# Strassen's seven products for the first product of a mixture-of-experts layer

## The chip, the cores and the metric

The kernel runs on one core of a Trainium2 chip. The metric is the device time of one execution, in microseconds (us). A core has a matrix engine (TensorE, PE in the profile, with its weight loads as PEld), a vector engine (VectorE, DVE), an activation engine (ScalarE, ACT), GpSimd (POOL), and SyncE (SP), whose queue issues most of the DMA transfers. Matmuls write to PSUM, which has eight banks; VectorE and ScalarE take the results from there to SBUF.

## The reference

Attention over pooled keys gives 2304 tokens of 512 features; a first gated layer follows, and then the second layer, which the change is about:

```python
def _moe2_ref(x, w_gate, w1, w2) -> np.ndarray:
    N, D = x.shape
    E = w_gate.shape[1]
    logits = x @ w_gate
...
    for _ in range(8):
        P /= P.sum(1, keepdims=True) + 1e-09
        P /= P.sum(0, keepdims=True) + 1e-09
        P *= N / E
    out = np.zeros((N, D), dtype=np.float32)
    for e in range(E):
        h = np.maximum(x @ w1[e], 0.0)
        ye = h @ w2[e]
        out += P[:, e:e + 1] * ye
    return out.astype(np.float32)
```

N is 2304, D is 512, there are E = 8 experts, and the hidden width F is 1024. All experts see all tokens. The first product is `x @ w1[e]`, the second `h @ w2[e]`.

## The kernel before, in words

Every float32 product is made of three passes. An operand is held as `hi + lo`, and `PASSES` names hi·hi, hi·lo and lo·hi. Making such a pair takes one ScalarE copy (hi) and one subtraction on VectorE or GpSimd (lo).

Tokens are cut into `NBLK` = 6 blocks of `TB` = 384, each of `TPB` = 3 tiles of 128. The program's order is written out by hand: each engine works through its own queue in the order of the code, and waits at an instruction hold up all that is behind it on that engine.

**First layer** (line 665 on, 72 steps): while it runs, attention goes on in stages, and the first two blocks also round the weights from float64. After each block, `x2_step` (lines 548 to 578) leaves the layer's result in `x2[j]`, and `gate_logits` (lines 583 to 603) makes the second layer's gate logits from it, in stages: one ScalarE copy and one GpSimd subtraction over 1536 columns, twelve small matmuls, three transposes.

**Second layer** (lines 794 to 828): 48 units, (expert e, block j) with the expert outside, and in each eight steps f, one for 128 hidden features; 384 steps. A step makes the first product for 384 tokens in one `gv` bank (12 matmuls of 384 columns: four slices of D, three passes, line 270), then ScalarE's Relu (line 806) and VectorE's rest (line 807), and the second product of the step before, in three `big` banks (9 matmuls of 512 columns, line 764), which is summed in PSUM over all eight f. At a unit's end three VectorE instructions (line 779) add the result, times the token's weight, to `acc`. `stream` loads weight chunks on SP's queue and splits them (lines 240 and 245); each is loaded once. `split_x` (lines 615 and 616) splits the next unit's block of `x2` anew.

The gate's softmax and its eight rounds of normalisation (`sinkhorn`, lines 714 to 748) are one stage per step of the first two units. A round has two halves: a product with `ones` on TensorE (line 739) sums over the partitions, and nine VectorE instructions stand between one such product and the next.

Of the kernel before, what the change touches and what calls it, by code (L numbers as in the profile page):

```python
# [8 lines left out]
F32 = mybir.dt.float32  # L9
# [10 lines left out]
def attention_moe_moe_kernel(  # L20
# [27 lines left out]
    E, _, FF2 = moe2_w1.shape  # L48
# [9 lines left out]
    TB = 384  # L58
# [4 lines left out]
    NF2 = FF2 // 128  # L63
    ROUNDS = 8
# [4 lines left out]
    base = ctx.enter_context(tc.tile_pool(name="base", bufs=1))  # L69
# [13 lines left out]
    x2 = {j: const.tile([128, KT, TB], F32, name=f"x2_{j}") for j in range(2)}  # L83
# [5 lines left out]
    def cols_of(w, f):  # L89
        return w[:, f * 128 : (f + 1) * 128].rearrange("(k p) f -> p k f", p=128)  # L90

    def rows_of(w, f):
        return w[f * 128 : (f + 1) * 128, :]
# [25 lines left out]
    NWA = 8  # L119
    wsplit = {}  # L120
# [9 lines left out]
    def load_wide():  # L130
# [5 lines left out]
        t = base.tile([128, KT * TB], U32, tag="x2", name="wide", bufs=NWIDE)  # L136
# [53 lines left out]
    def source(i):  # L190
        """Of a chunk of the first layer: its number among the rounded, and whether it
        is that one's first use."""
        kind, j, f = chunks[i][0]
        return 3 * f + "gvo".find(kind), j == 0

    def load_chunk():
        """Loads the next chunk that is not rounded on the way."""
# [11 lines left out]
        if i < n_moe1:
            nc.sync.dma_start(out=t, in_=narrow[source(i)[0]])  # L210
        elif kind == "1":
            nc.sync.dma_start(out=t.rearrange("p (k f) -> p k f", f=128), in_=cols_of(w, f))
        else:
            nc.sync.dma_start(out=t, in_=rows_of(w, f))
# [3 lines left out]
    def split_chunk():  # L218
        """Splits the next chunk; False where there is none, or no room for it."""
# [3 lines left out]
        m, first = source(i) if i < n_moe1 else (None, False)  # L223
# [5 lines left out]
        if i >= n_moe1 and (i - n_moe1) % (2 * NF2) < 2 * NF2 - NWA:  # L229
# [3 lines left out]
        if pool is None or in_use[tag] >= bufs:  # L233
            return False
# [633 lines left out]
```

## Time and profile before

| | |
|---|---|
| runs | 2297.35 us median of three, 2296.33 to 2297.91 |
| profiled execution | span 2291.2 us; its own time is not listed apart from the span. The median of the runs is 6.2 us above the span |
| TensorE busy | 96 % of the span, 11453 matmuls |
| VectorE, ScalarE, GpSimd busy | 40 %, 29 %, 15 % |
| granted TensorE clock, mean | 0.979 of 2.4 GHz |
| start of the second layer | its first product starts at about 670 us |

The page gives each engine's busy time, and then the span in 40 slices with a digit for the busy share in tenths. A stage table gives the same for stretches that one chooses. In the timeline a line is an instruction or a merged run of equal ones: start, duration, engine, source line, operation, output and inputs, and in brackets how long the engine had been idle and what ended that. Matmuls are pipelined, so that the distance between starts, and not the duration shown for one, is what a matmul costs.

### The profile page before, as it was taken

Reading aid. Unit: us, or ns where it says so; the run is one execution under the profiler, and the core shown is the slowest. Engines: PE = TensorE matmul, PEld = TensorE weight load, DVE = VectorE, ACT = ScalarE, POOL = GpSimd, SP = SyncE. Lnnn points to the kernel's source line nnn. Section 1 sums busy time; section 2 is a strip of 40 time slices with the busy share of each in tenths; the row PEclk is TensorE's granted clock in tenths of the full one; section 3 lists DMA queues with packets and bytes.
Section 4 is the critical chain, followed back from the end, with each engine's and each line's share of the span. In section 5 each row is a group of like instructions: output and inputs, shape, how many; then the busy total and the mean of one; then the engine's idle time right before and its main releaser. Section 6 shows DMA issues by size and latency. Waiting matters only on the chain.

```text
span 2291.2 us, 28161 instructions
## 1 busy us (share of the span) xinstructions
PE 2189.2 (96%) x11453; PEld 2002.6 (87%) x11453; DVE 919.0 (40%) x1510; ACT 663.8 (29%) x1342; POOL 351.3 (15%) x258
## 2 busy tenths in 40 slices
PE   4668899999999999999999999999999999999999
PEld 3657789999998999999999999999999999999998
DVE  7877965543345223224222322422332242223222
ACT  5345455544442122113111211311221131112111
POOL 5645635544530000000000000000000000000000
PEclk7779899999999999999999999999999999999999
DMA  8554444333340001002000100200020020001111
GB/s 220 152 164 151 138 118 124 116 119 106 121 134 14 1 22 52 1 1 74 1 1 19 56 1 1 74 1 1 15 59 1 1 74 1 1 15 33 28 28 28
DMA packets 115858, 129.77 MB, mean 57 GB/s; under 512 B 26384, under 2 KB 71440, under 8 KB 115728
## 3 DMA queue, kind: packets, MB, share of 16 engines
q1 hardware_dynamic: 110544, 118.53, 17.7%
q10 hardware_dynamic: 5184, 9.44, 1.1%
q8 instruction: 89, 1.46, 0.3%
q14 instruction: 41, 0.34, 0.0%
HBM read 113.79 MB, written 14.16 MB: 56 GB/s over the span
## 4 chain that ended last, share of the span: by engine, by line
PE 88%; DVE 6%; issue 2%; ACT 2%; POOL 1%; DMA 1%; SPq 0%; ACTq 0%; POOLq 0%; DVEq 0%
PE gv L270 46%; PE big L764 35%; PE big L558 5%; DVE made L174 1%; DVE sum L324 1%; PE at L398 1%; DVE wa_lo L245 1%; POOL wa_lo L245 1%; PE at L270 1%; DVE made L173 1%; PE at L469 1%; DVE wide L177 0%; PE at L455 0%; DMA kv<-in_k_dram 0%; DVE g L693 0%
## 5 line engine op out<-in xcount | busy, mean ns | idle before, releaser
L270 PE MATMUL gv<-xs,wa_hi 128*128 128x384 f32 x2688 | 701.6, 342 | 18.8 <-DVE g L693 9.6
L807 DVE SCALAR_TENSOR_TENSOR h<-gv,h 128x384 fp32r<-128x384 f32 x384 | 214.0, 557 | 1041.5 <-ACT h L806 1041.0
L806 ACT ACTIVATE h<-gv 128x384 fp32r<-128x384 f32 x384 | 188.9, 492 | 1202.3 <-PE gv L270 1202.3
L270 PEld LDWEIGHTS gv<-xs,wa_hi 128*128 128x128 f32 x2688 | 493.5, 191 | 41.3 <-issue 11.1
L270 PE MATMUL gv<-xs,wa_lo 128*128 128x384 f32 x1344 | 457.2, 340 | 11.4 <-POOL wa_lo L245 8.9
L270 PE MATMUL gv<-xs,wb_hi 128*128 128x384 f32 x1536 | 393.1, 336 | 0.0
L764 PE MATMUL big<-wb_hi,h 128*128 128x512 f32 x1152 | 389.9, 392 | 0.0
L764 PE MATMUL big<-wa_hi,h 128*128 128x512 f32 x1152 | 389.7, 392 | 0.0
L270 PEld LDWEIGHTS gv<-xs,wb_hi 128*128 128x128 f32 x1536 | 282.0, 188 | 16.4
L270 PEld LDWEIGHTS gv<-xs,wa_lo 128*128 128x128 f32 x1344 | 255.9, 190 | 13.1 <-POOL wa_lo L245 9.9
L270 PE MATMUL gv<-xs,wb_lo 128*128 128x384 f32 x768 | 259.1, 337 | 0.0
L764 PEld LDWEIGHTS big<-wa_hi,h 128*128 128x128 f32 x1152 | 216.1, 188 | 40.4
L764 PEld LDWEIGHTS big<-wb_hi,h 128*128 128x128 f32 x1152 | 216.3, 188 | 40.2
L764 PE MATMUL big<-wb_lo,h 128*128 128x512 f32 x576 | 227.5, 395 | 0.0
L764 PE MATMUL big<-wa_lo,h 128*128 128x512 f32 x576 | 227.5, 395 | 0.0
L245 DVE TENSOR_TENSOR wa_lo<-stage,wa_hi 128x512 fp32r<-128x512 f32 x148 | 134.4, 920 | 77.1 <-ACT wa_hi L240 65.4
L245 POOL TENSOR_TENSOR wa_lo<-stage,wa_hi 128x512 fp32r<-128x512 f32 x96 | 142.3, 1506 | 115.8 <-ACT wa_hi L240 102.3
L558 PE MATMUL big<-h,wa_hi 128*128 128x384 f32 x576 | 150.8, 342 | 0.3 <-DVE h L697 0.3
L240 ACT ACTIVATE wa_hi<-stage 128x512 fp32r<-128x512 f32 x244 | 140.8, 622 | 34.6 <-PE big L764 33.6
L270 PEld LDWEIGHTS gv<-xs,wb_lo 128*128 128x128 f32 x768 | 144.0, 188 | 0.0
L764 PEld LDWEIGHTS big<-wb_lo,h 128*128 128x128 f32 x576 | 108.0, 187 | 18.2
L764 PEld LDWEIGHTS big<-wa_lo,h 128*128 128x128 f32 x576 | 108.0, 187 | 18.2
(136 smaller groups left out, 1696.0 us busy)
## 6 DMA issues: line engine op xcount, KB each, us to landing
stage<-narrow SPq DMA_DIRECT2D x180, 256.0 KB
stage<-in_moe_w_dram SPq DMA_DIRECT2D x128, 256.0 KB
narrow<-made ACTq DMA_DIRECT2D x36, 256.0 KB
wide<-in_moe_w_gate_dram SPq DMA_DIRECT2D x12, 512.0 KB
wide<-in_moe_w_val_dram SPq DMA_DIRECT2D x12, 512.0 KB
wide<-in_moe_w_out_dram SPq DMA_DIRECT2D x12, 512.0 KB
kv<-in_k_dram SPq DMA_DIRECT2D x16, 288.0 KB
qraw<-in_q_dram SPq DMA_DIRECT2D x24, 192.0 KB
```

What stands on the lines that cost most here:

```text
L173: nc.vector.tensor_scalar(out=x, in0=high, scalar1=0x80000000, scalar2=None, op0=ALU.bitwise_and)
L174: nc.vector.scalar_tensor_tensor(out=x, in0=high, scalar=3, in1=x, op0=ALU.logical_shift_left, op1=ALU.bitwise_or)
L240: nc.scalar.activation(out=hi, in_=raw, func=AF.Copy)
L245: eng.tensor_tensor(out=lo, in0=raw, in1=f32(hi), op=ALU.subtract)
L270: nc.tensor.matmul(out=out_, lhsT=a[s], rhs=b[m], start=(i == 0), stop=(i == n - 1))
L324: nc.vector.tensor_reduce(out=s, in_=t.rearrange("p h j d -> p h d j"), axis=AX.X, op=ALU.add)
L398: nc.tensor.matmul(out=pt[:RP, 2 * i * SP : 2 * (i + 1) * SP], lhsT=qt[r][:, hp], rhs=kb[:, hp].rearrange("p i s -> p (i s)"), start=True, ...
L469: nc.tensor.matmul(out=po[64 * i : 64 * i + 64, h // 2 - 2 * g], lhsT=vs[:, h], rhs=a_ts[u][:, h].rearrange("p r s -> p (r s)"), start=Tru ...
L558: nc.tensor.matmul(out=x2p[d][:, :TB], lhsT=w[s][:, d * 128 : (d + 1) * 128], rhs=gs[j, f][m], start=(first and i == 0), stop=(last and i ...
L764: nc.tensor.matmul(out=yp[n][t], lhsT=a[s][:, cs], rhs=w[m], start=(f == 0 and i == 0), stop=(f == NF2 - 1 and i == 2),)
L806: nc.scalar.activation(out=hi, in_=pt[:, :TB], func=AF.Relu)
L807: nc.vector.scalar_tensor_tensor(out=lo, in0=pt[:, :TB], scalar=0.0, in1=f32(hi), op0=ALU.max, op1=ALU.subtract)
```

## The change

The second layer's loops are turned around: three pairs of token blocks outside, then the experts, then q = 0 to 3, which names a pair of hidden slices (q and q + 4): 96 steps instead of 384. In a step the first product is a 2 by 2 block product: hidden slice (`fh`) by half of D on the weights' side, half of D by block of tokens on the other. It is computed with one level of Strassen's algorithm (in Winograd's form): seven products of 6 matmuls of 384 columns, P1 to P7, instead of eight.

- **Tokens' side:** `after_block` takes the place of `gate_logits`. After an odd block it also makes three sums of blocks and splits them; seven split operands per pair of blocks go to DRAM (`fx_store`), and come back when the pair is worked on (`load_xf`, 768 KB each): for the next pair, each right after its operand's last product in the pair before.
- **Weights' side:** `prep_w1` makes, in every step, four sums on GpSimd (256 columns each), splits three blocks and four sums on ScalarE and GpSimd; `prep_w2` splits two slices of w2 on ScalarE and VectorE. All weights are loaded and split again for each pair: 1 MB per step. On the host, w1 is laid out so that a step's four blocks are contiguous.
- **Results:** P1, then P1+P6, P1+P6+P7 and P1+P6+P7+P4 are summed in one `at` bank, read in between by ScalarE copies (`c1`, `c2`) and a VectorE sum; three VectorE additions combine the others. A step makes four hidden tiles.
- **Second product:** six `y_chunk`s of 6 matmuls of 512 columns, of the step before, stand between the products. Each ends in a VectorE instruction that adds to `acc`, in every step and no longer once per expert.
- **Order:** `slot2` stands seven times in a step, and emits a stage of the gate or of `sinkhorn`, one of `prep_w1` and one of `prep_w2`. In step 0 there is no second product yet. `more` is a pool on the memory of `base`, which ends there.

```diff
+    NPAIR = NBLK // 2
+    CPP = 2 * TPB
+    QF = NF2 // 2
+    FX = 4 * TB
...
+    def fx_tile(dtype, name):
+        return xring.tile([128, 2, 2, TB], dtype, tag="fx", name=name, bufs=NWIDE)
+    def fx_split(src, eng):
+        t = fx_tile(F32R, "fx")
+        nc.scalar.activation(out=t[:, 0], in_=src, func=AF.Copy)
+        eng.tensor_tensor(out=t[:, 1], in0=src, in1=f32(t[:, 0]), op=ALU.subtract)
+        return t
+    def fx_store(t, p, i):
+        nc.sync.dma_start(out=xd[p][i], in_=f32(t).rearrange("p s k c -> p (s k c)"))
...
+    def after_block(j):
+        p, odd = divmod(j, 2)
+        fx = [fx_split(x2[j][:, 0:2], nc.gpsimd)]
+        yield
+        fx.append(fx_split(x2[j][:, 2:4], nc.gpsimd))
+        yield
+        pt = side_bank()
+        mm(
+            pt[:E, :TB],
+            [
+                ((wg_hi[:, kk], wg_lo[:, kk]), tuple(fx[kk // 2][:, s, kk % 2] for s in range(2)))
...
+        )
         nc.vector.tensor_copy(out=lt, in_=pt[:E, :TB])
...
+        if odd:
+            fx_store(fx[1], p, 2)
+        else:
+            fx_store(fx[0], p, 0)
+            fx_store(fx[1], p, 1)
...
+        if not odd:
             return
...
+        yield "logits"
+        a, b = x2[j - 1], x2[j]
+        tt = fx_tile(F32, "tt")
+        sub = nc.vector.tensor_sub
+        sub(out=tt[:, 0], in0=b[:, 0:2], in1=a[:, 0:2])
+        sub(out=tt[:, 1], in0=b[:, 2:4], in1=tt[:, 0])
+        yield
+        t1 = fx_split(tt[:, 0], nc.gpsimd)
+        yield
+        t2 = fx_split(tt[:, 1], nc.gpsimd)
+        fx_store(t1, p, 3)
+        yield
...
+        t4 = fx_split(tt[:, 1], nc.gpsimd)
...
+        t3 = fx_split(tt[:, 0], nc.gpsimd)
+        fx_store(t4, p, 5)
...
+        fx_store(t3, p, 6)
...
+    steps2 = [(p, e, q) for p in range(NPAIR) for e in range(E) for q in range(QF)]
...
+    def load_w1(n):
...
+            raw1[n] = pools["late"].tile([128, 4, 2, 128], F32, tag="raw1", name="raw1", bufs=2)
+            nc.sync.dma_start(out=raw1[n].rearrange("p a k f -> p (a k f)"), in_=moe2_w1[e, q])
+    def load_w2(n):
...
+            raw2[n] = pools["more"].tile([128, 2, DM], F32, tag="raw2", name="raw2", bufs=2)
+            nc.sync.dma_start(
+                out=raw2[n], in_=moe2_w2[e].rearrange("(h g p) d -> g p h d", h=2, p=128)[q]
+            )
+    def prep_w1(n):
...
+        raw = raw1.pop(n)
+        pool = pools["more" if n % 2 else "late"]
+        a11, a12, a22, a21 = (raw[:, i] for i in range(4))
+        ss = pools["late"].tile([128, 4, 2, 128], F32, tag="ss", name="ss", bufs=1)
+        s1, s2, s4, s3 = (ss[:, i] for i in range(4))
+        pl = nc.gpsimd.tensor_tensor
+        fa = pool.tile([128, 2, 3, 2, 128], F32R, tag="fa", name="fa", bufs=1)
+        fs = pool.tile([128, 2, 4, 2, 128], F32R, tag="fs", name="fs", bufs=1)
+        wsum[n] = fa, fs
+        nc.scalar.activation(out=fa[:, 0], in_=raw[:, 0:3], func=AF.Copy)
+        pl(out=s1, in0=a21, in1=a22, op=ALU.add)
+        pl(out=s3, in0=a11, in1=a21, op=ALU.subtract)
+        yield
+        pl(out=s2, in0=s1, in1=a11, op=ALU.subtract)
+        pl(out=s4, in0=a12, in1=s2, op=ALU.subtract)
+        yield
+        nc.scalar.activation(out=fs[:, 0], in_=ss, func=AF.Copy)
+        pl(out=fa[:, 1], in0=raw[:, 0:3], in1=f32(fa[:, 0]), op=ALU.subtract)
+        yield
+        pl(out=fs[:, 1, 0:2], in0=ss[:, 0:2], in1=f32(fs[:, 0, 0:2]), op=ALU.subtract)
+        pl(out=fs[:, 1, 2:4], in0=ss[:, 2:4], in1=f32(fs[:, 0, 2:4]), op=ALU.subtract)
+        yield
+    def prep_w2(n):
...
+        t = pools["more"].tile([128, 2, 2, DM], F32R, tag="w2hl", name="w2hl", bufs=2)
+        w2hl[n] = t
+        for i in range(2):
+            nc.scalar.activation(out=t[:, 0, i], in_=raw[:, i], func=AF.Copy)
+            nc.vector.tensor_sub(out=t[:, 1, i], in0=raw[:, i], in1=f32(t[:, 0, i]))
+            yield
...
+    def load_xf(p, i):
+        if p < NPAIR:
+            xf[p, i] = pools["late"].tile([128, 2, 2, TB], F32R, tag=f"xf{i}", name=f"xf{i}", bufs=1)
+            nc.sync.dma_start(out=f32(xf[p, i]).rearrange("p s k c -> p (s k c)"), in_=xd[p][i])
...
                 pools["late"] = ctx.enter_context(tc.tile_pool(name="late", bufs=1, reuse_waits="tile"))
+                load_w1(0)
+                load_w1(1)
+                first_w = prep_w1(0)
+            if j == NBLK - 1 and 2 <= f < 9:
+                load_xf(0, (0, 3, 4, 2, 6, 1, 5)[f - 2])
+            if j == NBLK - 1 and f >= NF1 - 4:
+                next(first_w, None)
...
-                    gate = gate_logits(prev[0])
+                    gate = after_block(prev[0])
...
-            if j == NBLK - 1 and f >= NF1 - KT:
-                split_x(0, f - NF1 + KT)
...
+        PRODUCTS = {
+            "P1": ((0, 0), 0),
+            "P2": ((0, 1), 1),
+            "P3": ((1, 2), 2),
+            "P4": ((0, 2), 5),
+            "P5": ((1, 0), 3),
+            "P6": ((1, 1), 4),
+            "P7": ((1, 3), 6),
+        }
+        def product(n, name, pt, start):
+            (which, i), x = PRODUCTS[name]
+            w = wsum[n][which]
+            t = xf[steps2[n][0], x]
+            m = 0
+            for k in range(2):
+                for s, o in PASSES:
                     nc.tensor.matmul(
-                        out=yp[n][t],
-                        lhsT=a[s][:, cs],
-                        rhs=w[m],
-                        start=(f == 0 and i == 0),
-                        stop=(f == NF2 - 1 and i == 2),
+                        out=pt[:, :TB],
+                        lhsT=w[:, s, i, k],
+                        rhs=t[:, o, k],
+                        start=(start and m == 0),
+                        stop=(m == 5),
+                        skip_group_check=True,
                     )
...
+        def hidden(n, fh, half, src):
+            t = pools["more"].tile([128, 2, TB], F32R, tag=f"h{fh}{half}", name=f"h{fh}{half}", bufs=2)
+            hs[n, fh, half] = t
+            nc.scalar.activation(out=t[:, 0], in_=src, func=AF.Relu)
+            nc.vector.scalar_tensor_tensor(
+                out=t[:, 1], in0=src, scalar=0.0, in1=f32(t[:, 0]), op0=ALU.max, op1=ALU.subtract
             )
...
+        def y_chunk(n, t):
...
+            p, e, q = steps2[n]
+            half, i = divmod(t, TPB)
+            cs = slice(i * 128, (i + 1) * 128)
+            py = bank("big", 4)
+            m = 0
+            for fh in range(2):
+                h = hs[n, fh, half]
+                for s, o in PASSES:
+                    nc.tensor.matmul(
+                        out=py, lhsT=h[:, s, cs], rhs=w2hl[n][:, o, fh], start=(m == 0), stop=(m == 5)
+                    )
+                    m += 1
...
+            if e == 0 and q == 0:
+                acc[t] = pools["more"].tile([128, DM], F32, tag="acc", name="acc", bufs=CPP + 2)
+                if p == 0:
+                    nc.vector.tensor_copy(out=acc[t], in_=py)
+                else:
+                    nc.vector.tensor_scalar_mul(out=acc[t], in0=py, scalar1=pr)
+            elif e == 0 and p == 0:
+                nc.vector.tensor_tensor(out=acc[t], in0=py, in1=acc[t], op=ALU.add)
+                if q == QF - 1:
+                    unscaled.append((t, pr))
...
+                while unscaled:
+                    u, pu = unscaled.pop(0)
+                    nc.vector.tensor_scalar_mul(out=acc[u], in0=acc[u], scalar1=pu)
+                nc.vector.scalar_tensor_tensor(
+                    out=acc[t], in0=py, scalar=pr, in1=acc[t], op0=ALU.mult, op1=ALU.add
+                )
+            if (e, q) == (E - 1, QF - 1):
+                for p0, np_, rows in out_rows(tt * 128):
+                    nc.sync.dma_start(out=rows, in_=acc[t][p0 : p0 + np_])
...
+        for n, (p, e, q) in enumerate(steps2):
+            last_of_pair = (e, q) == (E - 1, QF - 1)
+            pa = bank("at", 2)
+            pc = bank("gv", 2)
+            pb = bank("gv", 2)
+            product(n, "P1", pa, True)
+            if n == 0:
+                product(n, "P5", pc, True)
+                x2_step(*prev)
+                base_pool.__exit__(None, None, None)
+                pools["more"] = ctx.enter_context(
...
+                )
+                load_w2(0)
+                gate = after_block(NBLK - 1)
+                sk = sinkhorn()
+            load_w2(n + 1)
+            load_w1(n + 2)
+            prep = prep_w1(n + 1)
+            prep2 = prep_w2(n)
+            def slot2():
+                global_stage()
+                next(prep, None)
+                next(prep2, None)
+            def global_stage():
+                if n < QF + 2:
+                    if not sk_on:
+                        if next(gate, None) == "logits":
+                            sk_on.append(True)
+                    elif next(sk, "end") == "end":
+                        next(gate, None)
+            c1 = c_tile()
+            nc.scalar.copy(out=c1, in_=pa[:, :TB])
...
+            y_chunk(n - 1, 3)
+            slot2()
+            if n > 0:
+                product(n, "P5", pc, True)
+            c5 = c_tile()
+            nc.scalar.copy(out=c5, in_=pc[:, :TB])
...
+            y_chunk(n - 1, 4)
+            slot2()
+            product(n, "P6", pa, False)
+            c2 = c_tile()
...
+            y_chunk(n - 1, 5)
+            slot2()
+            product(n, "P3", pc, False)
+            nc.vector.tensor_tensor(out=pc[:, :TB], in0=pc[:, :TB], in1=c2, op=ALU.add)
+            hidden(n, 0, 1, pc[:, :TB])
...
+            slot2()
+            product(n, "P7", pa, False)
+            nc.vector.tensor_tensor(out=c5, in0=pa[:, :TB], in1=c5, op=ALU.add)
+            hidden(n, 1, 1, c5)
...
+            y_chunk(n - 1, 0)
+            slot2()
+            product(n, "P2", pb, True)
+            nc.vector.tensor_tensor(out=pb[:, :TB], in0=pb[:, :TB], in1=c1, op=ALU.add)
+            hidden(n, 0, 0, pb[:, :TB])
...
+            y_chunk(n - 1, 1)
+            slot2()
+            product(n, "P4", pa, False)
+            hidden(n, 1, 0, pa[:, :TB])
...
+            y_chunk(n - 1, 2)
+            slot2()
+        for t in (3, 4, 5, 0, 1, 2):
+            y_chunk(len(steps2) - 1, t)
...
+        if name == "moe2_w1":
+            a = a.reshape(8, 2, 2, 128, 2, 4, 128).transpose(0, 5, 3, 4, 1, 2, 6)
+            a = np.stack([a[:, :, :, f, k] for f, k in ((0, 0), (0, 1), (1, 1), (1, 0))], axis=3)
+            a = np.ascontiguousarray(a.reshape(8, 4, 128, 1024))
```

## Rows read from the trace of the kernel before

**Rows 1.** The page: span, busy times, and the slices of two rows

```profile
span 2291.2 us, 28161 instructions
PE 2189.2 (96%) x11453; PEld 2002.6 (87%) x11453; DVE 919.0 (40%) x1510; ACT 663.8 (29%) x1342; POOL 351.3 (15%) x258
...
POOL 5645635544530000000000000000000000000000
PEclk7779899999999999999999999999999999999999
```

**Rows 2.** Stage table: start, end and length, each engine's busy time (count), clock, DMA

```profile
200.00:300.00 100.00, 80.81 (x467) 76.27 (x466) 87.05 (x115) 50.78 (x93) 60.11 (x40) 0.88 0.47 145
...
1200.00:1600.00 400.00, 400.00 (x2008) 362.50 (x2007) 120.06 (x211) 85.47 (x176) 0.00 (x0) 1.00 0.07 22
```

**Rows 3.** Timeline of TensorE in the second layer: where each group of matmuls begins

```profile
1301.66 0.39 PE L764 MATMUL big<-wa_hi,h 128*128 128x512 f32 x1
...
1303.75 0.51 PE L270 MATMUL gv<-xs,wa_hi 128*128 128x384 f32 x2
...
1305.85 0.39 PE L764 MATMUL big<-wa_hi,h 128*128 128x512 f32 x1
...
1307.93 0.51 PE L270 MATMUL gv<-xs,wa_hi 128*128 128x384 f32 x2
```

**Rows 4.** Waits from 720 us on: us in total, times, longest

```profile
ACT h L806 <- PE gv L270: 1171.2, 373, 3.7
DVE h L807 <- ACT h L806: 1031.8, 369, 3.6
```

**Rows 5.** Groups by line: busy us, mean ns of one, idle before

```profile
L807 DVE SCALAR_TENSOR_TENSOR h<-gv,h 128x384 fp32r<-128x384 f32 x384 | 214.0, 557 | 1041.5 <-ACT h L806 1041.0
L806 ACT ACTIVATE h<-gv 128x384 fp32r<-128x384 f32 x384 | 188.9, 492 | 1202.3 <-PE gv L270 1202.3
...
L615 ACT ACTIVATE xs<-x 128x384 fp32r<-128x384 f32 x192 | 99.0, 516 | 0.0
...
L779 DVE SCALAR_TENSOR_TENSOR acc<-big,prob,acc 128x512 f32<-128x512 f32 x126 | 86.5, 742 | 1.7 <-PE big L764 1.7
...
L245 DVE TENSOR_TENSOR wb_lo<-stage,wb_hi 128x512 fp32r<-128x512 f32 x64 | 44.0, 692 | 33.8 <-ACT wb_hi L240 33.8
...
L240 ACT ACTIVATE wb_hi<-stage 128x512 fp32r<-128x512 f32 x64 | 39.7, 627 | 33.6 <-PE big L764 33.6
...
L587 POOL TENSOR_TENSOR xs<-x,xs 128x1536 fp32r<-128x1536 f32 x6 | 21.0, 3498 | 50.0 <-ACT xs L586 50.0
...
L577 ACT COPY x<-big 128x384 f32<-128x384 f32 x16 | 7.3, 480 | 2.8 <-PE big L558 2.6
...
L573 DVE TENSOR_TENSOR x<-x,big 128x384 f32<-128x384 f32 x8 | 3.9, 545 | 0.0
```

**Rows 6.** Timeline of POOL and of DVE in the first layer, around 400 us

```profile
400.80 0.46 POOL L327 TENSOR_TENSOR sum<-kv 72x128 f32<-72x128 f32 x1
401.22 5.01 POOL L245 TENSOR_TENSOR wa_lo<-stage,wa_hi 128x512 fp32r<-128x512 f32 x4
...
400.81 5.97 DVE L245 TENSOR_TENSOR wa_lo<-stage,wa_hi 128x512 fp32r<-128x512 f32 x1 [0.68 <-POOL kv L327]
```

**Rows 7.** Timeline of one half round of the normalisation, on PE and DVE

```profile
703.46 0.28 PE L739 MATMUL at<-cs,ones 128*128 128x8 f32 x2
...
707.84 0.28 PE L739 MATMUL at<-cs,ones 128*128 128x8 f32 x2
...
703.77 0.17 DVE L740 TENSOR_SCALAR cs<-at 128x8 f32<-128x8 f32 x1 [1.06 <-PE at L739]
...
705.95 0.44 DVE L736 TENSOR_REDUCE cs<-prob 128x8 f32<-128x144 f32 x1
```

**Rows 8.** The DMA's rate in 40 slices of 440 to 470 us

```profile
GB/s 249 259 139 265 33 0 0 0 0 0 0 11 0 0 0 49 292 60 251 380 16 0 87 262 27 240 393 71 0 0 0 0 0 55 284 82 254 358 16 0
```

**Rows 9.** The output's last transfers, as SP issues them

```profile
2285.09 3.10 SPq L789 DMA_DIRECT2D out_dram<-acc  x6
```

More of the change, by code (lines that the diff above doesn't have):

```diff
@@ L68, in attention_moe_moe_kernel @@
     const = ctx.enter_context(tc.tile_pool(name="const", bufs=1))
-    base = ctx.enter_context(tc.tile_pool(name="base", bufs=1))
+    xring = ctx.enter_context(tc.tile_pool(name="xring", bufs=1))
+    base_pool = tc.tile_pool(name="base", bufs=1, side="right")
+    base = base_pool.__enter__()
     dram = ctx.enter_context(tc.tile_pool(name="dram", bufs=1, space=DRAM))
@@ L82, in attention_moe_moe_kernel @@
     wg_lo = const.tile([128, KT, E], F32R, name="wg_lo")
-    x2 = {j: const.tile([128, KT, TB], F32, name=f"x2_{j}") for j in range(2)}
+    lt = const.tile([E, TB], F32, name="lt")
+    x2 = {}
     def f32(ap):
         return ap.bitcast(F32)
[L89 to L93, printed above, removed]
     def words(w):
@@ L119, in attention_moe_moe_kernel @@
     NWA = 8
+    xd = [[dram.tile([128, FX], F32, name=f"xd{p}_{i}") for i in range(7)] for p in range(NPAIR)]
     wsplit = {}
@@ L135, in load_wide @@
         kind, f, w = wide_src[i]
-        t = base.tile([128, KT * TB], U32, tag="x2", name="wide", bufs=NWIDE)
+        t = xring.tile([128, KT * TB], U32, tag="fx", name="wide", bufs=NWIDE)
         t = t[:, 0:1024].rearrange("p (c w) -> p c w", w=2)
@@ L203, in load_chunk @@
             return False
-        if i < n_moe1 and source(i)[0] >= n_used[0]:
+        if source(i)[0] >= n_used[0]:
             return False
         n_load[0] += 1
-        (kind, _, f), w = chunks[i]
         t = base.tile([128, 512], F32, tag="stage", name="stage", bufs=NST)
[L209 to L214, printed above, removed]
+        nc.sync.dma_start(out=t, in_=narrow[source(i)[0]])
         staged[i] = t
@@ L222, in split_chunk @@
             return False
-        m, first = source(i) if i < n_moe1 else (None, False)
+        m, first = source(i)
         if first:
@@ L569, in x2_step @@
         if j not in x2:
-            x2[j] = base.tile([128, KT, TB], F32, tag="x2", name=f"x2_{j}", bufs=NWIDE)
+            x2[j] = xring.tile([128, KT, TB], F32, tag="x2", name=f"x2_{j}", bufs=2)
         for d in range(KT):
@@ L603, in gate_logits @@
         yield
-    units = [(e, j) for e in range(E) for j in range(NBLK)]
-    xs2 = {}
-    def split_x(n, kk):
-        if n >= len(units):
+        if not odd:
             return
-        if kk == 0:
-            xs2[n] = xs_tile()
-        j = units[n][1]
-        hi, lo = (t[:, kk] for t in xs2[n])
-        nc.scalar.activation(out=hi, in_=x2[j][:, kk], func=AF.Copy)
-        nc.vector.tensor_sub(out=lo, in0=x2[j][:, kk], in1=f32(hi))
+        yield "logits"
+        a, b = x2[j - 1], x2[j]
@@ L710, in attention_moe_moe_kernel @@
         late = pools["late"]
-        acc = [late.tile([128, TPB, DM], F32, name=f"acc{j}") for j in range(NBLK)]
         def sinkhorn():
@@ L748, in sinkhorn @@
                 )
[L750 to L751 removed]
+        acc = {}
         hs = {}
[L753 to L790 removed]
@@ L792, in attention_moe_moe_kernel @@
-        last = prev
-        prev = None
-        for n, f in steps:
-            e, j = units[n]
-            w = wsplit["1", e, f]
-            xs = xs2[n]
-            pt = bank("gv", 2)
-            mm(
-                pt[:, :TB],
-                [(tuple(t[:, kk * 128 : (kk + 1) * 128] for t in w[:2]), tuple(t[:, kk] for t in xs)) for kk in range(KT)],
-            )
-            if j == NBLK - 1:
-                drop(("1", e, f))
-            hi, lo = h_tiles()
-            nc.scalar.activation(out=hi, in_=pt[:, :TB], func=AF.Relu)
-            nc.vector.scalar_tensor_tensor(
-                out=lo, in0=pt[:, :TB], scalar=0.0, in1=f32(hi), op0=ALU.max, op1=ALU.subtract
-            )
-            hs[n, f] = (hi, lo)
-            if prev is not None:
-                y_step(*prev)
-            else:
-                x2_step(*last)
-                gate = gate_logits(NBLK - 1)
-            prev = (n, f)
-            stream(2)
-            if 2 <= f < 2 + KT:
-                split_x(n + 1, f - 2)
-            if n < 2 and next(gate, "end") == "end":
-                next(sk, None)
-            if e == 1 and f == 1:
-                for t in range(TPB):
-                    tt = j * TPB + t
-                    nc.vector.tensor_scalar_mul(
-                        out=acc[j][:, t], in0=acc[j][:, t], scalar1=prob[:, tt, 0:1]
-                    )
```

118 lines of the change are left out of this document (58 added, 60 removed).

## The prediction

> **What bounds the kernel now.** I read the page's busy times first: TensorE is busy 96 % of a span of 2291.2 us, no other engine over 40 % [rows 1]. A busy TensorE need not be a TensorE at its pace, so next the stage table and the timeline of the second layer. In 400 us there run 2008 matmuls, 0.199 us each, with no idle time, at clock 1.00 [rows 2]; the timeline resolves them: nine of 512 columns start over 2.09 us (0.232 us each), twelve of 384 over 2.10 and 2.08 us (0.174 us each) [rows 3]. The price per column is equal for both, 0.00045 us, so a matmul costs its columns and nothing beside. Third the waits: ScalarE waits 1171 us for the products, VectorE 1032 us for ScalarE [rows 4]. From 670 us on, TensorE's columns alone set the time: 384 steps of 4.18 us are 1606 of the 1621 us that are left of the span. Only removed columns, or new holes in TensorE's stream, can move the end.
>
> **The change, part by part.** All sums are changes of the profiled execution; its span lies 6.2 us under the median of the runs, which is what the front table has, and I let those 6.2 us stand.
>
> *Removed columns.* The first product had 384 x 12 = 4608 matmuls of 384 columns; now it has 96 x 42 = 4032. The second keeps 96 x 36 = 3456. So 576 x 0.174 = **100.2 us** go [rows 3]. The groups change more often, 13 in a step against 8 in the same work before; the two distances for twelve matmuls differ by 0.02 us, so this costs at most 5 x 0.02 x 96 = 10 us; I take 0, as most rows show no extra. The Trainium skill (TensorE: Matmul & The Clock Gate, section Back-to-back issue gap) gives a gap of N/2.4 + 2.5 ns, 162.5 ns for 384 columns; by an estimate from it 93.6 us would go, and the time would be 7 us higher than mine. The rows measure the pace in this very loop, and decide.
>
> *One step in steady state.* On TensorE 42 x 0.174 + 36 x 0.232 = 15.66 us. Does the rest fit? VectorE: three additions out of PSUM at 0.545, four Relu rests at 0.557, six additions to `acc` at 0.742, two splits of w2 at 0.692 [rows 5]: 9.7 us, 62 %. ScalarE: three copies at 0.480, four Relus at 0.492, two splits at 0.627, and splits of 768 and 1024 columns, by the slope from 0.516 (384) to 0.627 us (512) some 0.85 and 1.07: 6.6 us. GpSimd: 512 columns take 1.25 us, 128 take 0.46 [rows 6], so 256 about 0.72; 768 are half of 3.50 [rows 5]: 4 x 0.72 + 1.75 + 2 x 1.25 = 7.1 us. All fit under 15.66 us. An addition whose result goes to PSUM has no row; between 0.545 and twice that a step gains 1.1 us of VectorE's time, which fits too.
>
> In-order chains matter more than sums. P6 may overwrite P1's bank only after the copy `c1`: the copy is ready 0.5 us after P1, and 1.39 us of second product and 1.04 us of P5 lie between. P3 waits for `c5`, P7 for `c2`, each with over 1 us to spare. The narrowest is P4, which needs VectorE's reading of the bank after P7: P3 ends 8.35 us into the step, then addition, Relu, rest, reading: 0.545 + 0.49 + 0.557 + 0.545, done at about 10.6; P4 starts at 13.2. That is 2.5 us of cover; if it is gone, TensorE waits. I take **0**.
>
> *DMA.* Loads rise to 1 MB per step, 67 GB/s; bursts reached 393 GB/s [rows 8]. At a change of pair seven loads of 0.79 MB stand on SP's queue, each issued when its last product is done and needed 14.6 us later. With the step's 1 MB that is 6.5 MB, 17 us at that rate, while the last is needed 29 us after the first could start. Each load waits on SP for a product, and behind it stand only the next loads, wanted a step later. I take 0; at half the rate some 5 us at each of two changes.
>
> *Step 0.* Here the second product's cover is missing. After `x2_step` ends (time 0) TensorE has P6, then the gate's twelve matmuls, then P3. Those matmuls need the second split of `x2` from GpSimd; that needs a ScalarE copy which stands behind the copy of w2's first slice, which waits for a load that can be issued only when `base` is free. A load takes about 4.4 us: 0.4 to issue, 1.3 for 512 KB at 393 GB/s, and 3.0 to land, as the last output transfer does (issues end at 2288.2, the span at 2291.2) [rows 1, 9]. So: w2's copy to 5.0, `c5` 5.5, x2's copy 6.3, GpSimd's half of 3.50 us to 8.1. P6 ends at 1.8: a hole of 6 us. Later in step 0 the normalisation's first transpose waits on VectorE behind the Relu rests, some 3 us more. I take **+9.7**; between 0 (the buffers are free early, all is hidden) and 15.
>
> *The normalisation.* Half a round is 2.62 us of VectorE, from 703.77 to 706.39, between two products with `ones` that lie 4.38 us apart now, so it is hidden [rows 7]. Now a stage comes every 2.57 us (P of 1.04, chunk of 1.39, the product itself 0.14), and once after 1.18. Each stage, TensorE waits until VectorE has done the chain of the last, before which stand an addition to `acc` (0.74) and, in four of seven segments of step 1, the additions and rests of a hidden tile. With the segments of step 1 in order, I find holes of 0.9, 0.9, 2.4, 1.7, 2.5, 2.5, 1.4 = 12.3 us. GpSimd now works beside it, 45 % of the time; two of the nine VectorE instructions take both inputs from SBUF and may find it in an operation, with 0.45 us left of it on average (first rival): 18 x 0.45 x 0.45 = 3.7. I take **+16**; between 3 (only the excess of 2.62 + 0.28 over 2.57 counts, nine times) and 28 (the holes twice as long, and 3.7).
>
> *Clock.* From 200 to 300 us TensorE is busy 81 % and the granted clock is 0.88 on average, below the upper level of 2.4 GHz; where it is busy throughout, 1.00 [rows 2]. The first two steps will look like the former: 12 % of some 30 us, **+3.6**, between 0 and 8.
>
> *First layer.* `after_block` adds, after an odd block, four splits of 768 columns (GpSimd 1.75 us each), one per step of 6.3 us, where GpSimd is at 4 to 5 tenths [rows 1]; its stores on SP wait for splits emitted a step earlier. Covered by weights split ahead; **+2**, between 0 and 8. What ran there for the second layer before (`split_x`, chunks) was hidden. At the end the last transfers stay: 0.
>
> **Sum:** -100.2 + 9.7 + 16 + 3.6 + 2 = -69, and 2297.35 - 69 = **2228 us**.
>
> **The rivals.**
>
> *GpSimd starves VectorE (slower).* At 400.81 us a VectorE subtraction with both inputs in SBUF, 0.692 us alone, took 5.97 us, and ended just as GpSimd's unbroken run from 400.80 to 406.23 did [rows 5, 6]. The second layer had no GpSimd work; now it has 7.1 us a step. If VectorE stands still while GpSimd runs, a step takes 9.7 + 7.1 = 16.8 us, 1.1 more than TensorE's 15.66: 2228 + 96 x 1.1 = 2338. It decides from 0.72 us per step on (69/96). Against it: of VectorE's fifteen instructions only three (two splits of w2, the rest of `c5`) take both inputs from SBUF, and in the first layer VectorE was busy 87 and GpSimd 60 of 100 us [rows 2], so they mostly run side by side. The Trainium skill (SBUF — State Buffer, section Who interferes with whom) says that a VectorE instruction with two SBUF inputs and a GpSimd instruction that reads SBUF block each other fully, the second one until the first is done; by its one-instruction form the loss would be 1.25 us at most each time, which the 5.97 us do not bear out.
>
> *Starved a little.* Only those three are held up, for runs of GpSimd of up to 5.4 us (two splits and the next step's sums); where that falls on P4's 2.5 us of cover, TensorE waits 0.2 to 0.6 us a step: 2247 to 2286, middle 2266. For it: the long row; against it: by my order GpSimd runs mostly after VectorE's reading of P7.
>
> *No holes.* The start is hidden as now: only columns go and the low bounds stay: -100.2 + 3 = 2200.
>
> **How the numbers follow.** Forecast 0.66, no holes 0.08, starved a little 0.15, starved 0.11. The forecast with its costs at their ends runs from 2200 to 2256 (15 + 28 + 8 + 8 = 59 instead of 31); the range reaches into the third case, **2199 to 2275**, and leaves out the fourth and a part of the third. A measurement of this kernel can tell 0.2 % (4.6 us) from no change. Faster by more: 0.66 + 0.08 + 0.12 = 0.86; within: 0.03; slower: 0.11.
>
> **What would show it.** After: 10877 matmuls, 576 fewer; in a stretch of the second layer TensorE busy throughout, groups of six 384-column matmuls over 1.04 us, steps of 15.7 us; holes in the first 40 us of the layer, their releasers GpSimd's split, then VectorE's `cs`. A steady step above 16 us, with TensorE waiting on VectorE after P7, makes the forecast wrong, as would waits for `xf` at two places.

## The result, and the profile after

The changed kernel takes 2219.95 us (median of four runs, 2217.51 to 2221.6), the kernel before beside it 2296.84 us. The ratio is 0.9665, 95 % interval 0.9652 to 0.9679: 77 us faster. The forecast was 2228 us.

The page after, with the lines that answer to [rows 1]:

```profile
span 2215.7 us, 28889 instructions
PE 2097.0 (95%) x10877; PEld 1904.1 (86%) x10877; DVE 1445.4 (65%) x2102; ACT 926.6 (42%) x1712; POOL 1106.9 (50%) x948
...
POOL 6555635744653645454444545454545444444541
PEclk7879899999998999999999999999999999999999
```

576 matmuls are gone, VectorE's busy time is up by 526 us and GpSimd's by 756 us, now in every slice; TensorE is still the engine that has no room. The stage table, as in [rows 2] (columns as there; the four stretches of 20 us begin where the second layer does):

```profile
670.00:690.00 20.00, 14.20 (x72) 11.35 (x70) 6.83 (x13) 7.96 (x14) 12.98 (x11) 0.91 0.54 171
690.00:710.00 20.00, 13.54 (x59) 10.97 (x60) 15.15 (x44) 6.87 (x11) 8.06 (x8) 0.90 0.14 50
710.00:730.00 20.00, 17.40 (x73) 14.73 (x74) 17.07 (x53) 5.31 (x10) 0.16 (x1) 0.85 0.01 5
730.00:750.00 20.00, 16.83 (x72) 14.85 (x71) 14.31 (x18) 7.68 (x14) 18.79 (x14) 0.83 0.43 160
...
1200.00:1600.00 400.00, 400.00 (x1994) 359.47 (x1993) 266.19 (x382) 159.16 (x282) 192.07 (x177) 1.00 0.22 76
```

From 1200 to 1600 us TensorE has no hole at clock 1.00: 1994 matmuls in 400 us, 78 to a step, 15.65 us per step. The first 80 us of the layer hold the rest of the story: TensorE is busy 62 of 80 us, and the granted clock is 0.83 to 0.91. What TensorE waited for from 640 us to the end (us in total, times, longest us):

```profile
PE big L843 <- DVE cs L840: 7.4, 6, 3.1
PE big L265 <- POOL fx L585: 4.0, 2, 2.8
PE at L880 <- DVE c L1002: 3.2, 1, 3.2
PE big L826 <- DVE m L824: 2.9, 1, 2.9
PE at L880 <- ACT c L975: 0.4, 1, 0.4
```

These are eleven waits, 17.9 us, all before 742 us. The one behind `c` stands out. The timeline of TensorE, and of VectorE before it:

```profile
741.05 2.29 PE L880 MATMUL at<-xf,fa 128*128 128x384 f32 x6 [3.17 <-DVE c L1002]
...
736.13 2.46 DVE L642 TENSOR_TENSOR tt<-x,tt 128x768 f32<-128x768 f32 x1
738.51 2.01 DVE L643 TENSOR_TENSOR tt<-x 128x768 f32<-128x768 f32 x1
740.45 0.55 DVE L1002 TENSOR_TENSOR c<-at,c 128x384 f32<-128x384 f32 x1
```

P4 (line 880) waits for the reading after P7 (line 1002), which stands behind two sums of token blocks of `after_block`. Its six matmuls then take 2.29 us and not 1.20: from 741 to 745 us the granted clock is 0.50, the lower level of 1.2 GHz.

**The account.** The second layer runs from its first product to the end of the span: 670.51 to 2291.2 us before, 1620.7 us; 671.30 to 2215.7 after, 1544.4: 76.3 us less. The steady steps alone saved more. By the counts of [rows 2] a step of the kernel before, 21 matmuls, took 400 x 21 / 2008 = 4.183 us, and 384 of them 1606.4; now 96 steps of 400 x 78 / 1994 = 15.647 us take 1502.1. So 104.3 us arrived and 28.0 were given back, 17.5 of them as waits (17.9 less 0.4 before). Of the other 10.5 us, 8.7 are the lower clock, by an estimate from TensorE's timeline: the groups between 682 and 748 us that ran below a granted clock of 1.00, each against the same group in a steady step. What is left, the restarts after the waits among it, no run takes apart.

### The profile page after: what moved, and what is told of

It is laid out like the page before. It is cut to its first block, busy times and chain, and to the rows that moved or that the text cites. A ratio compares the mean times of both kernels' runs of the same rounds, so it can differ in the third digit from the quotient of the medians.

```text
span 2215.7 us, 28889 instructions
## 1 busy us (share of the span) xinstructions
PE 2097.0 (95%) x10877; PEld 1904.1 (86%) x10877; DVE 1445.4 (65%) x2102; ACT 926.6 (42%) x1712; POOL 1106.9 (50%) x948
## 3 DMA queue, kind: packets, MB, share of 16 engines
q8 instruction: 85, 1.39, 0.3%
## 4 chain that ended last, share of the span: by engine, by line
PE 85%; DVE 7%; POOL 3%; issue 3%; ACT 2%; DMA 1%; SPq 0%; ACTq 0%; POOLq 0%; DVEq 0%
PE big L911 36%; PE at L880 18%; PE gv L880 13%; PE gv L265 10%; PE big L553 5%; DVE made L178 1%; POOL wa_lo L239 1%; PE at L393 1%; DVE sum L319 1%; PE at L464 1%; DVE wa_lo L239 1%; PE at L265 0%; DVE made L177 0%; POOL fx L585 0%; PE at L450 0%
## 5 line engine op out<-in xcount | busy, mean ns | idle before, releaser
L911 PE MATMUL big<-w2hl,h 128*128 128x512 f32 x3456 | 895.4, 395 | 0.0
L911 PEld LDWEIGHTS big<-w2hl,h 128*128 128x128 f32 x3456 | 643.0, 188 | 102.8
L931 DVE SCALAR_TENSOR_TENSOR acc<-big,prob,acc 128x512 f32<-128x512 f32 x540 | 403.4, 747 | 282.3 <-PE big L911 276.1
L265 PE MATMUL gv<-xs,wa_hi 128*128 128x384 f32 x1152 | 309.4, 350 | 19.4 <-DVE g L800 10.4
L880 PE MATMUL at<-xf,fa 128*128 128x384 f32 x1152 | 235.3, 339 | 3.2 <-DVE c L1002 3.2
L265 PEld LDWEIGHTS gv<-xs,wa_hi 128*128 128x128 f32 x1152 | 212.0, 195 | 26.0 <-DVE g L800 10.8
L880 PE MATMUL at<-xf,fs 128*128 128x384 f32 x1152 | 233.3, 337 | 0.4 <-ACT c L975 0.4
L880 PE MATMUL gv<-xf,fs 128*128 128x384 f32 x1152 | 232.0, 336 | 0.0
L707 DVE TENSOR_TENSOR w2hl<-raw,w2hl 128x512 fp32r<-128x512 f32 x192 | 226.0, 1177 | 2.3 <-ACT w2hl L706 2.3
L265 PE MATMUL gv<-xs,wa_lo 128*128 128x384 f32 x576 | 198.8, 345 | 13.9 <-POOL wa_lo L239 11.6
```

What stands on the lines that cost most here:

```text
L265: nc.tensor.matmul(out=out_, lhsT=a[s], rhs=b[m], start=(i == 0), stop=(i == n - 1))
L707: nc.vector.tensor_sub(out=t[:, 1, i], in0=raw[:, i], in1=f32(t[:, 0, i]))
L880: nc.tensor.matmul(out=pt[:, :TB], lhsT=w[:, s, i, k], rhs=t[:, o, k], start=(start and m == 0), stop=(m == 5), skip_group_check=True,)
L911: nc.tensor.matmul(out=py, lhsT=h[:, s, cs], rhs=w2hl[n][:, o, fh], start=(m == 0), stop=(m == 5))
L931: nc.vector.scalar_tensor_tensor(out=acc[t], in0=py, scalar=pr, in1=acc[t], op0=ALU.mult, op1=ALU.add)
```

## The experiments

Eleven runs beside the kernel before. Each profile's second layer, measured as above:

| run | us, ratio (95 %) | second layer, us | TensorE's waits in it, us |
|---|---|---|---|
| changed kernel again (e0) | 2222.22, 0.9677 (0.9664 to 0.9690) | 1544.5 | 17.2 |
| spread stages (e3) | 2212.08, 0.9632 (0.9619 to 0.9646) | 1536.1 | 12.8 |
| step 0 (e4) | 2218.74, 0.9658 (0.9644 to 0.9671) | 1539.6 | 15.5 |
| both (e7) | 2212.84, 0.9635 (0.9622 to 0.9648) | 1535.5 | 13.6 |
| eight products (e1) | 2301.46, 1.002 (1.001 to 1.003) | 1628.6 | 8.5 |
| better order (e8) | 2205.67, 0.9609 (0.9593 to 0.9626) | 1529.5 | 10.6 |

The place where the second layer begins lies between 669.9 and 678.1 us in the profiles, and between 671.3 and 676.5 in those whose first layer is that of the changed kernel; so the layer's own length compares better than the medians.

**e0, the yardstick.** No edit. 

> The changed kernel again, as the yardstick for the runs beside it: 2217 to 2222 us, 0.9665 of the kernel before.

 2222.22 us, as expected.

**e1, Strassen undone, the new order kept.**

```diff
-            product(n, "P1", pa, True)
...
+                part(n, fh, half, kh, pts[which])
...
+        i = {(0, 0): 0, (0, 1): 1, (1, 1): 2, (1, 0): 3}[fh, kh]
```

> The new order of loops, the w2 and token operands through DRAM, and the second product as they are, but with the plain eight products in place of Strassen's seven: no sums of weights, no sums of token blocks, no combining additions, 48 matmuls of 384 columns per step for 42. Theory of the columns: the 576 matmuls come back at 0.174 us, 100 us, and the holes of the start, which the order brings, shrink a little with VectorE's lighter load: 2310 to 2322, so slower than the kernel before by the start's 15 to 25 us. Rival (the gain comes from the new order, which splits no token block anew and loads in long rows, and Strassen adds little): 2235 to 2290.

2301.46 us, no gain at all: the removed columns carry the gain, and the rival falls. But it is some 9 us under my range. The steady stretch is full, with VectorE busy only 51 % and GpSimd 15 %:

```profile
1190.00:1590.00 400.00, 400.00 (x2012) 362.06 (x2012) 205.58 (x288) 94.91 (x168) 61.09 (x48) 1.00 0.23 75
```

So the start is what differs: 8.5 us of waits for 17.9. Against the kernel before, the new order alone costs 1628.6 - 1620.7 = 8 us: its 96 steps of 400 x 84 / 2012 = 16.70 us take 1603.2, 3 less than before, and 11 are lost at the start. Strassen on top of it brings 1628.6 - 1544.4 = 84 us, 101 of columns less 17 of its own. I had put the start's price down to the order; some three fifths of it, 17 of 28 us, come with Strassen's additions, sums and GpSimd work. Which of these three it is, this run doesn't tell.

**e2, more GpSimd work.**

```diff
         pl(out=fs[:, 1, 0:2], in0=ss[:, 0:2], in1=f32(fs[:, 0, 0:2]), op=ALU.subtract)
         pl(out=fs[:, 1, 2:4], in0=ss[:, 2:4], in1=f32(fs[:, 0, 2:4]), op=ALU.subtract)
+        pl(out=fs[:, 1, 0:2], in0=ss[:, 0:2], in1=f32(fs[:, 0, 0:2]), op=ALU.subtract)
+        pl(out=fs[:, 1, 2:4], in0=ss[:, 2:4], in1=f32(fs[:, 0, 2:4]), op=ALU.subtract)
```

The subtraction for `fa` is doubled in the same way. 

> GpSimd makes each of a step's three subtractions twice (the same values again): 4.4 us more per step, 7.5 to 12 us. Theory of the cover: VectorE is held up longer at its three instructions with two inputs from SBUF, but the reading after P7 stays inside the 2.45 us before P4, or passes it by little: a step of 15.7 to 16.0 us, 2220 to 2255. Rival (GpSimd starves VectorE until TensorE waits): VectorE's 10.4 us with waits grow past 15.66, a step of 16.7 us and more, 2318 or above, TensorE waiting at P4 for the sum c.

2226.89 us, ratio 0.9699 (0.9686 to 0.9713). The stage table, and the group of w2's splits on VectorE, of this run and then of the changed kernel (1190 to 1590 us):

```profile
1190.00:1590.00 400.00, 400.00 (x1993) 359.34 (x1992) 283.80 (x382) 159.38 (x283) 312.36 (x255) 1.00 0.25 84
...
L710 DVE TENSOR_TENSOR w2hl<-raw,w2hl 128x512 fp32r<-128x512 f32 x52 | 83.7, 1609 | 0.0
```

```profile
L707 DVE TENSOR_TENSOR w2hl<-raw,w2hl 128x512 fp32r<-128x512 f32 x51 | 60.1, 1179 | 0.0
```

With GpSimd busy 78 % the splits of w2 take 1609 ns, where they took 1179 with GpSimd at 49 % and 692 without it [rows 5]. VectorE is held up, as the rival says, but in steady steps TensorE isn't: no wait of TensorE is left from 800 us on. The cover, the time between the end of VectorE's reading and the P4 that needs it, takes it all. The price is paid at the start: the second layer is 1551.3 us long, 6.8 more than in e0, and TensorE waits 20.4 us in it, 3.2 more.

**e10 and e11, VectorE's reading put off.**

```diff
+            for _ in range(4):
+                nc.vector.tensor_tensor(out=extra, in0=pc[:, :TB], in1=c2, op=ALU.add)
```

and `range(6)`, after the hidden tile behind P3. 

> Four more VectorE additions per step (PSUM and c2 into a tile that nobody reads, 0.55 us each) between the rest of the hidden tile and the reading after P7. Theory of the cover (in a steady step the reading ends 2.45 us before P4 needs it, and only what passes that costs): 2.2 us fit, no steady wait; some 2 to 8 us at the start, where VectorE is full: 2223 to 2232. Rival (any lateness on VectorE is handed on to TensorE): 0.5 to 2.2 us a step, 2270 to 2430.

 

> Six such additions, 3.3 us. Theory of the cover: 3.3 - 2.45 = 0.85 us of waiting at P4 in every step for the sum c, 96 x 0.85 = 82 us, and 3 to 12 at the start: 2300 to 2318. Rival (only VectorE's sum counts, 10.4 + 3.3 = 13.7 us of a step of 15.66): no steady wait, 2223 to 2235.

Four: 2232.44 us, just above my range, ratio 0.9722 (0.9708 to 0.9737), and no wait of TensorE after 802 us. Its steady step is 15.69 us (1989 matmuls from 1190 to 1590 us), 0.04 more; the rest is the start, with 23.3 us of waits. Six: 2336.91 us, ratio 1.0181 (1.0164 to 1.0198). TensorE's waits of the six, and one step on VectorE and TensorE:

```profile
PE at L880 <- DVE c L1005: 85.4, 94, 4.5
```

```profile
1303.93 3.51 DVE L1000 TENSOR_TENSOR extra<-gv,c 128x384 f32<-128x384 f32 x6
...
1307.35 0.55 DVE L1005 TENSOR_TENSOR c<-at,c 128x384 f32<-128x384 f32 x1
...
1305.54 1.55 PE L911 MATMUL big<-w2hl,h 128*128 128x512 f32 x6
1307.95 1.31 PE L880 MATMUL at<-xf,fa 128*128 128x384 f32 x6 [0.85 <-DVE c L1005]
1309.10 1.55 PE L911 MATMUL big<-w2hl,h 128*128 128x512 f32 x6
```

There is a threshold, and it lies at 2.45 us of lateness: the six put the reading off by 3.42 us (1303.93 to 1307.35), 0.97 past the cover, and P4 starts 2.41 us after the chunk before it where a steady step has 1.39, so 1.02 late. That the idle time in the profile is the 0.85 that I had worked out from 3.3 us is partly chance: it is counted from the modelled end of the chunk (1307.09), 0.16 after the next group would have started. VectorE was busy 79 % then, so its sum bounds nothing. The price was larger than the idle time: 1860 matmuls in 400 us are 16.77 us per step, 1.12 more than 15.65. That is the 1.02, and 0.10 because P4's six matmuls take 1.15 us from start to start and not 1.05. The 0.27 beyond the idle time are 26 us over 96 steps, and carry 2300 to 2318 up to the 2337 measured.

**e5 and e9, the token operands' loads.** In e5 all seven `load_xf` calls stand after P4; e9 has them there in another order:

```diff
+                for i in (5, 0, 3, 4, 2, 6, 1):
+                    load_xf(p + 1, i)
```

> At both changes of pair all seven token operands are loaded after P4 of the pair's last step, no longer each after its own last product. Theory of the cover: the operand for P1 is then needed 1.4 us after it can be issued and takes some 5 us, and 5.5 MB at 390 GB/s need 14 us; TensorE waits 4 to 7 us at each change, 8 to 14 us in all: 2228 to 2236. Rival (the loads were already late or are not on the path): no change, 2218 to 2224.

2221.15 us, ratio 0.9678 (0.9664 to 0.9691), but this edit could not show anything. SP's timeline in e5, and in the changed kernel:

```profile
1191.57 13.55 SPq L715 DMA_DIRECT2D xf<-xd  x7
1205.21 0.39 SPq L669 DMA_DIRECT2D raw<-in_moe_w_dram  x1
```

```profile
1185.91 13.55 SPq L715 DMA_DIRECT2D xf<-xd  x7
1199.56 0.39 SPq L669 DMA_DIRECT2D raw<-in_moe_w_dram  x1
```

Nothing else is on SP's queue in between, so where the calls stand in the program changes nothing; each load waits for its own product as before. Only the order on the queue could. 

> At a change of pair the load of P4's operand now stands first of the seven on SP's queue, so that all wait for P4 of the pair's last step; the others follow in their order. Theory of the loads' cover (14.6 us from issue to need hide them): P1's operand is issued 0.8 us after P4's end and is the second of two transfers of 2 us, with 3 us to land; needed 1.4 us after P4. TensorE waits 5 to 9 us at each of two changes, partly again at P5 and P6: 2230 to 2244. Rival (the loads have slack in any order): no wait, 2217 to 2224.

2237.23 us, ratio 0.9741 (0.9727 to 0.9756). TensorE's timeline at the two changes of pair:

```profile
1210.77 2.29 PE L880 MATMUL at<-xf,fa 128*128 128x384 f32 x6 [4.93 <-DMA xf<-xd]
1719.80 2.29 PE L880 MATMUL at<-xf,fa 128*128 128x384 f32 x6 [5.02 <-DMA xf<-xd]
```

Two waits of 5 us, and after each P1 at the lower clock (2.29 us for 1.20), 15 us in all. So the loads are hidden because each is issued right behind its operand's last product, not because transfers are short.

**e3, e4, e7, the holes of the start.** e3 lets `sinkhorn` and the token sums go on in three of the seven slots; e4 loads w2's first slice in the first layer, issues both splits of `x2` first, and puts the gate's matmuls later, by the trace behind P7 (688.85 us) and not behind P4, as the expectation says; e7 has both.

```diff
+                elif 1 <= n < 3 * QF and n_slot[0] in (1, 3, 6):
+                    if next(sk, "end") == "end":
```
```diff
+            for _ in range(4):
+                yield
...
+                next(gate)
+                next(gate)
```

> The stages of the normalisation, and the sums of token blocks that come after them, stand in three of a step's seven slots (the first, third and sixth) from step 1 on, no longer in all seven from step 0 on. Theory of the holes (TensorE waits because a stage's chain of 2.6 us on VectorE doesn't fit between two neighbouring slots): the waits for the sums cs (7.4 us in six), for the maximum m (2.9) and for the reading after P7 (3.2, behind the token sums) go, and with them a part of the time at the lower clock, 13 to 18 us: 2202 to 2207. Rival (VectorE has a backlog in these steps whatever the order, so the waits move to the other slots): under 4 us, 2216 to 2220.

 

> Step 0 alone: its first slice of w2 is loaded during the first layer, both splits of the last block's x2 are issued straight after the first layer's last product, and the gate's twelve matmuls stand behind P4 and not behind P6. Theory of the holes: 0.45 + 1.15 + 2.83 = 4.4 us of waits in step 0 go, and some of the lower clock: 2212 to 2216. Rival (the holes only move, as the normalisation starts four slots later and falls into the fuller step 1): 2218 to 2224.

 

> The two edits of step 0 and of the spread stages together. Theory of the holes: nearly all 18 us of waits of the second layer go and most of the time at the lower clock, 18 to 26 us: 2194 to 2202, at least 2 us under the spread stages alone. Rival (the columns and a backlog set the time): 2214 or more.

e3 gains 10 us against e0, less than the 13 to 18 I expected; e4 3.5, little more than the 2.3 us by which the medians of the changed kernel and of e0, the same program, differ; and e7 no more than e3 alone, far from the 2194 to 2202 I expected. The waits for `cs` fall from 7.4 to 3.7 us in e3, but the reading after P7 comes late three times; by the order of the code the chain of the third slot's stage stands ahead of it. TensorE's waits in e3:

```profile
PE big L265 <- POOL fx L585: 4.0, 2, 2.8
PE big L843 <- DVE cs L840: 3.7, 2, 2.5
PE at L880 <- DVE c L1004: 3.7, 3, 1.9
```

In e4 GpSimd's split is no longer waited for, but P6 now waits for `c1`, which stands behind two splits on ScalarE, and the transposes for `lt` on VectorE:

```profile
683.64 1.31 PE L889 MATMUL at<-xf,fs 128*128 128x384 f32 x6 [1.95 <-ACT c L985]
...
695.08 0.44 PE L624 MATMUL big<-ident,lt 8*128 8x8 f32 x3 [2.94 <-DVE lt L615]
```

So for step 0 the rival holds, in the main: without the second product's matmuls there is nothing to cover its chains, and most of a hole closed opens at the next.

**e8, a better version.** Stages in slots 2, 5 and 7, the reading after P7 ahead of the hidden tile's rest, the last pair's token sums on GpSimd, `c1` first in step 0, the gate's matmuls behind P2.

```diff
-            hidden(n, 0, 1, pc[:, :TB])
...
             nc.vector.tensor_tensor(out=c5, in0=pa[:, :TB], in1=c5, op=ALU.add)
+            hidden(n, 0, 1, pc[:, :TB])
...
+                elif 1 <= n < 3 * QF and n_slot[0] in (2, 5, 7):
```

> All that the holes so far point to: the normalisation in slots 2, 5 and 7 of a step, the reading after P7 ahead of the hidden tile's rest on VectorE, the last pair's token sums on GpSimd, the first slice of w2 loaded early, and in step 0 the gate's matmuls behind P2 and its transposes two slots later. Theory of the holes: under 6 us of the 18 us of waits stay, and the clock stays up: 2198 to 2206. Rival (what is left is the rest of step 0, without cover whatever the order): 2208 to 2214.

2205.67 us, the fastest here, 17 us under e0 and 92 under the kernel before. The waits are still 10.6 us, more than the 6 I expected, but they are shorter, and from 690 to 790 us the clock stays at 1.00; of the 15 us by which the second layer is shorter than in e0, 6.6 are waits; the rest, the clock among it, was not taken apart.

## Why the prediction was right

**Columns.** The mechanism is right, the size 4 us too small: 104.3 us for 100.2. A steady step was to take 15.66 us and takes 15.65, and e1 shows that with eight products nothing is left of the gain. The 4 us come mostly from the step before, which took 4.183 us and not 12 x 0.174 + 9 x 0.232 = 4.176. More frequent changes of group cost nothing. By the gap that the Trainium skill states for a single matmul (TensorE: Matmul & The Clock Gate, section Back-to-back issue gap), 162.5 and 215.8 ns, a step would take 14.6 us, by an estimate. The trace does not agree: its 15.65 us are the pace of [rows 3], 174 and 232 ns.

**The steady step's cover.** Right. I had the reading after P7 done at 10.6 us, P4 at 13.2. The changed kernel's timeline:

```profile
1304.50 0.55 DVE L1002 TENSOR_TENSOR c<-at,c 128x384 f32<-128x384 f32 x1
...
1307.50 1.21 PE L880 MATMUL at<-xf,fa 128*128 128x384 f32 x6
```

From 1305.05 to 1307.50 are 2.45 us, and e10 and e11 measured this cover from both sides.

**Step 0.** +9.7 forecast; the waits there are 0.45 + 1.15 + 2.83 + 2.95 = 7.4 us. The engines are those named, GpSimd with its split of x2 and then VectorE behind the rests, but the cause of the split's lateness was another. I had it stand behind a load of w2 that could be issued only when `base` was free (and whose terms, 0.4, 1.3 and 3.0, add up to 4.7 and not 4.4 us). The changed kernel's timelines of SP, ScalarE and GpSimd:

```profile
669.28 0.38 SPq L669 DMA_DIRECT2D raw<-in_moe_w_dram  x1
...
678.29 0.85 ACT L584 ACTIVATE fx<-x 128x768 fp32r<-128x768 f32 x1
...
678.64 1.19 POOL L688 TENSOR_TENSOR ss<-raw 128x256 f32<-128x256 f32 x1
679.80 1.17 POOL L689 TENSOR_TENSOR ss<-raw 128x256 f32<-128x256 f32 x1
680.93 1.80 POOL L585 TENSOR_TENSOR fx<-x,fx 128x768 fp32r<-128x768 f32 x1
```

The load was issued at 669.28 us, before the layer began, and the copy for the second split was done at 679.14. GpSimd came to the split only at 680.93, since two sums of w1 stood before it on its own queue. So of e4's edits the earlier splits could count and the earlier load could not; apart they were not tested.

**The normalisation.** The cause was right, VectorE's chain between two products with `ones`; the term was too large: +16 forecast, 7.4 us of waits for `cs`. I had holes of 0.9, 0.9, 2.4, 1.7, 2.5, 2.5 and 1.4 us; they are 0.88, 0.77, 3.15, 0, 0.22, 1.76 and 0.62. Up to the third they are near. Behind it TensorE itself was slow:

```profile
709.56 0.60 PE L843 MATMUL big<-cs,ones 128*128 128x8 f32 x2 [3.15 <-DVE cs L840]
710.01 2.27 PE L880 MATMUL at<-xf,fs 128*128 128x384 f32 x6
712.08 2.76 PE L911 MATMUL big<-w2hl,h 128*128 128x512 f32 x6
714.64 0.43 PE L843 MATMUL big<-cs,ones 128*128 128x8 f32 x2
```

At a granted clock of 0.50 (710 to 714.5 us) it took 5.1 us from one product with `ones` to the next, 2.6 forecast, and VectorE's chain was done in that time: part of what is missing in the waits stands in the clock's term. The 3.7 us for GpSimd had little cause: from 710 to 730 us, where the last four of the holes were to be, it was busy 0.16 us (the stage table above).

**The clock.** +3.6 forecast, too small: 8.7 us by the estimate in the account. The share was right, the stretch too short: I had 12 % of 30 us, and over the four stretches of 20 us the granted clock is 0.87 on average. The holes go on to 742 us, and after each of the four of 2.8 to 3.2 us (at 682.78, 691.58, 709.56 and 741.05 us) whole groups run at the lower level.

**What I missed.** The sums of token blocks. I had counted `after_block`'s splits, in the first layer, as hidden; in the second layer its VectorE sums fell on P4's cover, which I had called the narrowest place, and P4 waited 3.2 us. Most of that goes with GpSimd's work. The first pair of these sums, on VectorE, and GpSimd's work during the second pair, which is shown above (736.13 and 738.51 us):

```profile
727.93 0.95 DVE L634 TENSOR_TENSOR tt<-x,x 128x768 f32<-128x768 f32 x1
728.91 0.96 DVE L635 TENSOR_TENSOR tt<-x,tt 128x768 f32<-128x768 f32 x1
...
735.92 1.85 POOL L695 TENSOR_TENSOR fa<-raw,fa 128x768 fp32r<-128x768 f32 x1
737.73 1.98 POOL L697 TENSOR_TENSOR fs<-ss,fs 128x512 fp32r<-128x512 f32 x1
739.67 1.99 POOL L698 TENSOR_TENSOR fs<-ss,fs 128x512 fp32r<-128x512 f32 x1
```

With GpSimd idle the sums took 0.95 and 0.96 us, beside its unbroken run 2.46 and 2.01. The difference, 2.6 us, is an estimate of what this hold-up has in the wait; no run takes it alone.

**First layer.** +2 forecast, 0.8 between the two profiles. One wait for GpSimd's `wa_lo` grew from 0.4 to 3.1 us, but with the same first layer its end scatters by 5.2 us from profile to profile, so the size stays open. The 6.2 us that I let stand between span and median were no constant either. Each time that is listed with its span is 1.7 to 2.1 us above it (2217.51 for the profile after), so that the profiled execution before lay some 4 us under its median.

**The rivals.** "GpSimd starves VectorE" was right on VectorE and wrong on the end: the hold-up is real (e2), and stays inside the cover in every steady step; it reached TensorE once, at 741 us. By the Trainium skill (SBUF — State Buffer, section Who interferes with whom) the two engines share a port pair under an exclusive lock, and whoever comes second waits. The steady step agrees: at 1313.26 us a split of w2 began 0.70 us into a GpSimd instruction of 1.85, and took 1.70 us for 0.68. (The long row that I had for this rival ended 0.55 us after GpSimd's run, at 406.78 us, and not with it.) "Starved a little" and "no holes" didn't come.

In sum -104.3 and +28.0 against -100.2 and +29.3 (without the first layer). The first part is right by its mechanism. That the second came within 2 us is luck: its waits were forecast at 25.7 us and measured at 17.5, the rest at 3.6 and measured at 10.5, and the two errors cancel.

## What to carry to other kernels

On an engine that is full, price a change in its columns first, and then ask of each instruction that it must wait for how late it may come; in e11 a reading 1.0 us too late cost 1.1 us a step, in e10 one that came 0.2 us early enough cost 0.04. Work that is added to idle engines is paid where the cover is missing, at the start, so look there for the second half of the gain. To move a transfer, change its place on the queue that issues it, not the place of its line in the program.

## What was not expected of the hardware

A wait costs more than its idle time: in e11 0.85 us of idle in the profile lengthened the step by 1.12 us, in steady state at clock 1.00. A GpSimd instruction is also held up by VectorE: its 512-column splits in the first steps took 1.98 us where they take 1.30 in steady steps, in the very stretch where the token sums ran on VectorE.
